# Attention and gated layer on one core: value products of 64 columns a head, two heads side by side in the array, x stored once

## Chip, cores and metric

The kernel runs on one core of a Trainium2 chip. The metric is the device time of one execution, in microseconds (us).

## What is computed

A relative-position attention over 4 batches, 8 heads, 576 positions and 64 values a head, and then a gated layer on its output, all in float32:

```python
# q, k, v: (4, 8, 576, 64)
scores = q @ k.T / 8 + bias        # bias: (8, 576, 576), a small network of the positions
attn = exp(scores - max); attn = attn / (sum(attn) + 1e-9)
x = (attn @ v).transpose(0, 2, 1, 3).reshape(2304, 512)
out = (sigmoid(x @ w_gate) * (x @ w_val)) @ w_out     # d_ff = 1536
```

## The kernel before

It has three stages one behind the other: the bias tables (to about 120 us), the attention (120 to 380 us), and the gated layer in two forms, three-term products for the first 768 tokens (380 to 535 us) and sums of seven products for the rest (535 to the end). Numbers that need more than one pass of the array are split into an upper and a lower part.

**The attention** runs over 16 units; a unit u is a pair of heads p of one batch b. Each unit has nine steps s, and the loop variable n counts steps over all units (n = 9u + s). `score(n)` makes two heads' scores in the even steps (L627, each head on 64 of the array's 128 rows) and the last 64 rows of both heads in step 8 (L616). `soft` takes the scores out of PSUM with the bias on VectorE (L643) and makes the exponential `en` on ScalarE (L648). `turn` brings `en` into `at`, transposed and split into two float16 parts: four blocks of the first head over TensorE and PSUM (L672, split by ScalarE L561 and VectorE L562), four of the second (`CROSS`, steps 1, 3, 5, 7) over GpSimd, which splits them into `cr` (L555, L666), and a transposing DMA on SP's queue (L667). `crp` holds three `cr` buffers. GpSimd also splits the next unit's k and q (L555, L566). `tail` in step 3 does the last 64 columns and, in `normal`, sends the row sums out (`rt`, L696).

**The value products** of a unit are done while the next unit runs. `products(u)` yields 36 matmuls: for each head and each half of the 576 rows nine with a stationary operand of 128 columns, 64 of the upper part of v and 64 of its lower part, so that `acc` holds two halves which have to be added. `FILL` says how many are taken in each step. ScalarE copies `acc` to `xe` (L736) and SP stores it to `xs` in DRAM, both halves (L741). `split_v` makes v's parts, the upper on ScalarE (L602), the lower on VectorE from two SBUF operands (L603), in the steps `VSTEP`.

**Around the change** the order on each engine is the order of the program (`manual_schedule`): SP takes its DMAs one behind the other and waits at each for what it needs. A transposing DMA of the block that is turned in step t is issued in step t + 2 + `XLAG`. What has to be loaded again is put in `loads` and issued a step or two later. From unit 12 on `Moe.ahead` slips loads and preparation of x for the gated layer into the steps (`PLAN`).

**The gated layer** loads x back from `xs`. For tokens below 768 `load_x` brings both halves and `prep_x` adds them (L900). For the others `x_do` loads one half ("l") and adds the other by a DMA that accumulates, issued by GpSimd ("+", L1057).

Of the kernel before, what the change touches and what calls it, by code (L numbers as in the profile page):

```python
# [22 lines left out]
NA = S // 4  # L23
HF = S // 2
NCH = S // 64
FILL = (0, 6, 3, 6, 3, 6, 3, 6, 3)
ENB = 11
WM = 6
LAG, WSTEP, VSTEP, TAIL = 2, 2, (5, 7), 3
KSTEP, QSTEP = 1, 4  # L30
EARLY = 2
YPOS = [18, 22, 26, 30, 34, 38, 46, 52, 57, 62, 67, 72], [3, 9, 15, 21, 27, 33, 39, 45, 52, 58, 66, 72]
# [46 lines left out]
TURN = (0, 0), (1, 0), (0, 1), (1, 1), (0, 2), (1, 2), (0, 3), (1, 3)  # L79
CROSS = (1, 3, 5, 7)  # L80
TERMS = (0, 0), (0, 1), (1, 0)
XLAG = 3
XE = True, True
UP = 14
VCHUNK = (3, 4, 5, 6, 7)
# [86 lines left out]
@with_exitstack  # L172
def tile_kernel(ctx, tc, q, k, v, small, w_gate, w_val, w_out, steps, lpos, xtab, lx, out, phases="0AB"):
    nc = tc.nc
    dram = ctx.enter_context(tc.tile_pool(name="dram", bufs=1, reuse_waits="tile", space=bass.MemoryType.DRAM))
    xs = dram.tile([H * 2 * D, NT], F32, name="xs")
    rs = dram.tile([H, NT], F32, name="rs")
    scratch = dram.tile([3 * DFF // 128, 128, 4, 128], F32, name="scratch")

    moe = Moe(tc, w_gate, w_val, w_out, scratch, xs, rs, out)  # L180
    with ExitStack() as right, ExitStack() as att:
        pool = lambda n, st, side: st.enter_context(tc.tile_pool(name=n, bufs=1, side=side, reuse_waits="tile"))
        first = right.enter_context(ExitStack())
        keep = pool("keep", att, "left")
        over = pool("over", first, "right")
        biasL = keep.tile([128, NP, S], F32, name="biasL")
        ident = keep.tile([128, 128], F32, name="ident")
        make_identity(nc, ident)
        biases = over.tile([128, 24, S], F32, name="bias0"), keep.tile([128, 8, S], F32, name="bias3")

        def extra(n):
            n -= 9 * B * (NP - 1)
            if n == EARLY:
                first.close()
                moe.early(right)
            if n >= EARLY:
                moe.ahead(n)

        sizes = {}
        attn = attention(tc, att, q, k, v, biases, biasL, ident, xs, rs, sizes, extra)  # L200
        next(attn)
        with tc.manual_schedule():
            bias(tc, v, small, steps, lpos, xtab, lx, biases, biasL, ident, keep, sizes, moe, lambda: next(attn))
        if "A" in phases:
            for _ in attn:
                pass
            att.close()
# [309 lines left out]
def attention(tc, att, q, k, v, biases, biasL, ident, xs, rs, sizes, extra):  # L517
# [9 lines left out]
    yield  # L527


    units = [(p, b) for p in range(NP) for b in range(B)]  # L530
    qkraw, vraw, vsplit = {}, {}, {}

# [18 lines left out]
    load_q(0)  # L551
    load_v(0)
    yield
    def copy(dst, src):
        nc.gpsimd.tensor_scalar(out=dst, in0=src, scalar1=1.0, scalar2=1.0, op0=ALU.mult, op1=ALU.mult)  # L555

    def half(ap):
        return ap.rearrange("p (a b) -> p a b", a=2)

# [29 lines left out]
    st = pool("st", 4)  # L589
    rtp = pool("rtp", 2)  # L590
    atp = pool("atp", 2)
    crp = pool("crp", 3)
    xep = pool("xep", 2)
    ps_t = pool("ps_t", 3, space=PSUM)
    ps_v = pool("ps_v", 1, space=PSUM)
    ps_s = pool("ps_s", 2, space=PSUM)

    def split_v(u, h):
        if h == 0:
            vsplit[u] = vp.tile([128, 2, 5, 2, D], F16, name="vv")  # L600
        t, vv = vraw[u][:, h], vsplit[u][:, h]
        nc.scalar.activation(out=vv[:, :, 0], in_=t, func=AF.Copy, scale=sizes["up"])  # L602
        return lambda: nc.vector.scalar_tensor_tensor(out=vv[:, :, 1], in0=t, scalar=sizes["up"], in1=vv[:, :, 0], op0=ALU.mult, op1=ALU.subtract)  # L603

    state = {}

# [83 lines left out]
    def normal(u, pt):  # L690
        p, b = units[u]
        nc.tensor.transpose(pt[0:9, 2], state[u][0], ident)
        rt = rtp.tile([9, 128], F32, name="rt")

        def leave():
            nc.vector.tensor_scalar(out=rt, in0=pt[0:9, 2], scalar1=sizes["out"][0:9], scalar2=None, op0=ALU.mult)  # L696
            to = rs[2 * p:2 * p + 2, S * b:S * b + S]
            nc.sync.dma_start(out=to[:, 0:512].rearrange("h (i p) -> h i p", p=128), in_=rt[0:8])
            nc.sync.dma_start(out=to[:, 512:576].rearrange("(o h) p -> o h p", o=1), in_=rt[8:9].rearrange("o (h p) -> o h p", h=2))

        return leave
# [10 lines left out]
    def products(u):  # L712
        p, b = units[u]
        sm, at, ens = state[u]
        for h in range(2):
            xe = xep.tile([128, S], F32, name="xe")
            for e in range(2):
                cs = slice(HF * e, HF * e + HF)
                if u < NU - 1:
                    acc = ps_v.tile([128, 512], F32, name="acc")  # L720
                else:
                    if e == 0:
                        pair = ps_s.tile([128, 2, 512], F32, name="sc")
                    acc = pair[:, e]
                vv = vsplit[u][:, h]
                mms = []
                for J in range(4):
                    w = vv[:, J].rearrange("p s d -> p (s d)")
                    mms += [(w, at[:, h, J, cs]), (w, at[:, h, 5 + J, cs])]
                mms.append((vv[:, 4].rearrange("p s d -> p (s d)"), at[:, h, 4, cs]))  # L730
                for i, (l, r) in enumerate(mms):
                    nc.tensor.matmul(out=acc[:, 0:HF], lhsT=l, rhs=r, start=(i == 0), stop=(i == len(mms) - 1))  # L732

                    def leave(xe=xe, cs=cs, acc=acc, h=h, e=e):
                        if XE[e]:
                            nc.scalar.activation(out=xe[:, cs], in_=acc[:, 0:HF], func=AF.Copy)  # L736
                        else:
                            nc.vector.tensor_copy(out=xe[:, cs], in_=acc[:, 0:HF])
                        if e == 1:
                            r = D * (2 * p + h)  # L740
                            nc.sync.dma_start(out=xs[2 * r:2 * r + 2 * D, S * b:S * b + S], in_=xe)  # L741

                    yield leave if i == len(mms) - 1 else None

    NU = len(units)
    crossed = []
    with tc.manual_schedule():
        work = iter(())
        after, late, due, loads = [], [], [], []
        for n in range(9 * NU + LAG + 1):  # L750
# [27 lines left out]
                work = products(u - 1)  # L778
            if n == 9 * NU + LAG - 1:
                work = products(u - 1)  # L780
            for _ in range(FILL[s] if n < 9 * NU else 9 if n < 9 * NU + LAG else 0):
                f = next(work, None)
                if f:
                    f()
            if s in VSTEP and u < NU:
                late.append(split_v(u, VSTEP.index(s)))
                if s == VSTEP[1] and u + 1 < NU:
                    loads.append(lambda z=u + 1: load_v(z))
            extra(n)
        for f in after + late:  # L790
            f()
# [5 lines left out]
class Moe:  # L797
# [82 lines left out]
    def load_x(self, c, kc, eng=None):  # L880
        ts = slice(self.T * c, self.T * c + self.T)
        t = self.pools["xin"].tile([128, 2, self.T], F32, name="xin")
        for e in range(2):
            (eng or self.nc.sync).dma_start(
                out=t[64 * e:64 * e + 64],
                in_=self.xs[256 * kc + 128 * e:256 * kc + 128 * e + 128, ts].rearrange("(s p) t -> p s t", s=2))
        return t

    def load_r(self, c, kc, eng=None):
# [6 lines left out]
    def prep_x(self, c, t, r, hi, lo, kc):  # L896
        nc = self.nc
        x = t[:, 0]

        return [lambda: XENG(nc, c).tensor_tensor(out=x, in0=x, in1=t[:, 1], op=ALU.add),  # L900
                lambda: nc.vector.tensor_tensor(out=x, in0=x, in1=r, op=ALU.mult),
                lambda: nc.scalar.activation(out=hi[:, kc], in_=x, func=AF.Copy),
                lambda: nc.vector.tensor_tensor(out=lo[:, kc], in0=x, in1=hi[:, kc].bitcast(F32), op=ALU.subtract)]
# [115 lines left out]
    def x_do(self, q, w):  # L1019
# [8 lines left out]
            c, k = 2 * q + (n[2] == "2"), kc + 2 * (n[1] == "2")  # L1028
        if what == "l":
            t[n] = self.xtile(q)  # L1030
            self.load_half(nc.sync, t[n], c, k, 0)
        elif what == "r":
            t[n, "rec"] = self.load_r(c, k)
        elif what == "+":
            self.load_half(nc.gpsimd, t[n], c, k, 1, accum_op=ALU.add)
        elif what == "*":
            nc.vector.tensor_tensor(out=t[n], in0=t[n], in1=t.pop((n, "rec")), op=ALU.mult)
        elif what == "s":
# [11 lines left out]
            nc.scalar.activation(out=var[n][:, 0, kc], in_=t[n], func=AF.Copy, scale=self.up[q])  # L1050
        else:
            nc.vector.scalar_tensor_tensor(out=var[n][:, 1, kc], in0=t[n], scalar=self.up[q], in1=var[n][:, 0, kc], op0=ALU.mult, op1=ALU.subtract)  # L1052

    def load_half(self, eng, t, c, k, s, **how):
        for e in range(2):
            r = 256 * k + 128 * e + 64 * s
            eng.dma_start(out=t[64 * e:64 * e + 64], in_=self.xs[r:r + 64, self.T * c:self.T * c + self.T], **how)  # L1057
# [299 lines left out]
```

## Time and profile before

| | |
|---|---|
| three runs | 805.39, 801.32, 805.51 us; median 805.39 |
| the profiled execution | 800.84 us, its span 799.0 us |
| busy in the span | TensorE 735.8, VectorE 650.3, ScalarE 555.4, GpSimd 360.1 us |
| TensorE's granted clock | 0.987 of full speed |
| HBM | 80.80 MB read, 23.67 MB written |

A span is the time from the first to the last instruction, and 1.84 us of the execution lie outside it. Times inside the trace are counted from the span's start. The matmuls' ends are modelled, so that busy TensorE is not TensorE at its peak.

### The profile page before, as it was taken

Reading aid. Unit: us, or ns where it says so; the run is one execution under the profiler, and the core shown is the slowest. Engines: PE = TensorE matmul, PEld = TensorE weight load, DVE = VectorE, ACT = ScalarE, POOL = GpSimd, SP = SyncE. Lnnn points to the kernel's source line nnn. Section 1 sums busy time; section 2 is a strip of 40 time slices with the busy share of each in tenths; the row PEclk is TensorE's granted clock in tenths of the full one; section 3 lists DMA queues with packets and bytes.
Section 4 is the critical chain, followed back from the end, with each engine's and each line's share of the span. In section 5 each row is a group of like instructions: output and inputs, shape, how many; then the busy total and the mean of one; then the engine's idle time right before and its main releaser. Section 6 shows DMA issues by size and latency. Waiting matters only on the chain. (4 is left out here: it accounts for less than half of the span.)

```text
span 799.0 us, 17293 instructions
## 1 busy us (share of the span) xinstructions
PE 735.8 (92%) x6343; PEld 539.5 (68%) x6343; DVE 650.3 (81%) x1362; ACT 555.4 (70%) x1206; POOL 360.1 (45%) x451
## 2 busy tenths in 40 slices
PE   7999879888888988777999999998999999999997
PEld 4898867666766766565899899974555555555553
DVE  6788879888888889996498998878988886877762
ACT  5888738787887878776666666577666667666652
POOL 2245349788879986973001110046733221533100
PEclk9999988999999999999999999999999999999999
DMA  5487315878888798898989863357522211422102
GB/s 199 149 202 175 116 59 119 190 181 168 178 174 186 184 185 208 204 220 207 320 259 257 260 172 107 108 148 190 175 80 80 80 53 57 155 80 80 54 1 80
DMA packets 137237, 121.86 MB, mean 153 GB/s; under 512 B 82368, under 2 KB 106048, under 8 KB 137152
## 3 DMA queue, kind: packets, MB, share of 16 engines
q1 hardware_dynamic: 130560, 112.03, 51.5%
q0 software_dynamic: 4672, 5.77, 5.0%
q10 hardware_dynamic: 1920, 2.95, 1.1%
q8 instruction: 50, 0.82, 0.4%
q14 instruction: 35, 0.29, 0.1%
HBM read 80.80 MB, written 23.67 MB: 131 GB/s over the span
## 5 line engine op out<-in xcount | busy, mean ns | idle before, releaser
L1158 PEld LDWEIGHTS <-wv 128*128 128x128 f16 x1008 | 98.0, 98 | 85.5 <-issue 10.7
L648 ACT ACTIVATE en<-en,mn 128x576 f32<-128x576 f32 x144 | 110.8, 774 | 24.7 <-DVE mn L643 22.6
L1116 POOL TENSOR_TENSOR ws<-wm 128x256 f32<-128x256 f32 x44 | 42.4, 964 | 157.2 <-DMA wm<-scratch 109.0
L1158 PE MATMUL pg<-xq,wv 128*128 128x384 f16 x576 | 109.3, 326 | 3.3 <-ACT c L1184 2.4
L643 DVE CUSTOM_DVE_ANT_0 en<-sc,bias 128x576 f32<-128x576 f32 x128 | 91.9, 755 | 21.5 <-PE sc L627 19.1
L732 PE MATMUL acc<-at,vv 128*128 128x288 f16 x540 | 84.1, 288 | 19.4 <-DVE at L562 10.7
L666 POOL TENSOR_TENSOR cr<-en,cr 128x512 f16<-128x512 f32 (+1 forms) x128 | 97.1, 779 | 5.3
L627 PEld LDWEIGHTS sc<-k,part 64*128 64x128 f32 x768 | 58.5, 189 | 43.1 <-DVE mn L643 16.5
L627 PE MATMUL sc<-k,part 64*128 64x288 f32 x768 | 78.3, 317 | 10.0 <-DVE mn L643 8.1
L1005 PE MATMUL po<-wo,gh 128*128 128x512 f16 x288 | 85.7, 379 | 0.0
L1158 PE MATMUL pu<-xq,wv 128*128 128x384 f16 x432 | 82.0, 326 | 2.1 <-DVE c L1164 2.1
L1057 POOL DMA_DIRECT2D xt<-xs x32 | 27.0, 1085 | 108.7 <-DMA xt<-xs 108.7
L1164 DVE TENSOR_TENSOR c<-pu,c 128x384 f32<-128x384 f32 x72 | 40.0, 555 | 42.5 <-PE pu L1158 28.7
L562 DVE SCALAR_TENSOR_TENSOR at<-pt,at 128x512 f16<-128x512 f32 (+3 forms) x128 | 69.5, 564 | 5.8 <-ACT at L561 4.8
L561 ACT ACTIVATE at<-pt 128x512 f16<-128x512 f32 (+3 forms) x128 | 60.1, 496 | 19.9 <-PE pt L672 19.8
L732 PEld LDWEIGHTS <-vv 128*128 128x128 f16 x576 | 56.2, 98 | 25.0 <-issue 9.3
L427 PE MATMUL bps<-cfs,ind 128*128 128x64 bf16 x1458 | 67.5, 193 | 3.5 <-DVE bias L443 1.8
L408 ACT ACTIVATE ind<-y 128x576 bf16<-128x576 f32 x100 | 62.4, 651 | 10.8 <-PE y L403 8.0
L427 PEld LDWEIGHTS <-ind 128*128 128x128 bf16 x1458 | 58.7, 98 | 9.7 <-issue 3.0
L555 POOL TENSOR_SCALAR cr<-en 128x576 f16<-128x576 f32 x64 | 45.3, 708 | 43.9 <-DMA at<-cr 32.8
L1176 ACT ACTIVATE gh<-c 128x384 f16<-128x384 f32 x48 | 25.1, 523 | 54.1 <-DVE c L1174 52.5
L672 PE MATMUL pt<-ident,en 128*128 128x128 f32 x320 | 53.3, 291 | 6.5 <-ACT en L648 6.4
(179 smaller groups left out, 1757.3 us busy)
## 6 DMA issues: line engine op xcount, KB each, us to landing
wm<-scratch SPq DMA_DIRECT2D x48, 256.0 KB
xs<-xe SPq DMA_DIRECT2D x32, 288.0 KB
scratch<-wm SPq DMA_DIRECT2D x27, 256.0 KB
wo<-scratch SPq DMA_DIRECT2D x24, 256.0 KB
qr<-in_q_dram SPq DMA_DIRECT2D x16, 320.0 KB
vr<-in_v_dram SPq DMA_DIRECT2D x16, 320.0 KB
kr<-in_k_dram SPq DMA_DIRECT2D x16, 288.0 KB
xrec<-rs SPq DMA_DIRECT2D x48, 96.0 KB
```

Source lines behind the costliest of these rows:

```text
L408: nc.scalar.activation(out=o, in_=y[:, :, 0:HF], func=AF.Sigmoid, scale=float(2.0 ** 64))
L427: nc.tensor.matmul(out=o, lhsT=st, rhs=cfs[:, part], start=(part == 0), stop=(part == 2))
L561: nc.scalar.activation(out=hi, in_=ps, func=AF.Copy, scale=float(2.0 ** UP))
L562: return lambda: nc.vector.scalar_tensor_tensor(out=lo, in0=ps, scalar=float(2.0 ** UP), in1=hi, op0=ALU.mult, op1=ALU.subtract)
L627: nc.tensor.matmul(out=pair[h][:, e, 0:HF], lhsT=qs[rows, l, 128 * it:128 * it + 128], rhs=ks[rows, r, HF * e:HF * e + HF], start=(i == 0) ...
L643: nc.vector.tensor_tensor_reduce(out=half(en), in0=ps[:, :, 0:HF], in1=half(nbias), scale=-0.125, scalar=3.0e38, op0=ALU.add, op1=ALU.min, ...
L648: nc.scalar.activation(out=en, in_=en, func=AF.Exp, bias=mn, scale=-1.0, accum_out=sm)
L666: nc.gpsimd.tensor_tensor(out=t[:, a:a + z.stop - z.start], in0=en[:, z], in1=t[:, z], op=ALU.subtract)
L672: nc.tensor.transpose(pt[:, J], en[:, 128 * J:128 * J + 128], ident)
L732: nc.tensor.matmul(out=acc[:, 0:HF], lhsT=l, rhs=r, start=(i == 0), stop=(i == len(mms) - 1))
L1005: self.nc.tensor.matmul(out=po, lhsT=l[:, tt], rhs=r, start=(first and i == 0), stop=(last and i == 2))
L1158: nc.tensor.matmul(out=p, lhsT=W[i][:, l, at + kc], rhs=V[b][:, r, kc], start=(new and n == 0), stop=(n == 5), skip_group_check=not new)
```

## The change

The stationary operand of a value product has 64 columns, upper or lower part, and the two heads of a pair write to the partitions 0 to 63 and 64 to 127 of the same `acc`. The three terms upper by upper, upper by lower and lower by upper are added up in PSUM, so that `acc` is x itself for two heads. A unit now has 56 matmuls in 28 pairs (7 in each of the steps 1, 3, 5, 7), two copies to `xe` and one store. `xs` has half the rows; nothing is added in the gated layer. The lower part of v is taken by VectorE from the raw v in SBUF and the upper part in PSUM, which TensorE puts there by a product with a float16 identity (`lower_v`). `rt` is made by ScalarE. There are four `cr` buffers, the transposing DMAs are issued a step earlier, and v is loaded later.

```diff
-FILL = (0, 6, 3, 6, 3, 6, 3, 6, 3)
+FILL = (0, 7, 0, 7, 0, 7, 0, 7, 0)
-LAG, WSTEP, VSTEP, TAIL = 2, 2, (5, 7), 3
+LAG, WSTEP, VSTEP, TAIL = 2, 2, (3, 5), 3
-XLAG = 3
+XLAG = 2
-    xs = dram.tile([H * 2 * D, NT], F32, name="xs")
+    xs = dram.tile([H * D, NT], F32, name="xs")
+    eye = per.tile([128, 128], F16, name="eye")
+    copy(eye, ident)
-    crp = pool("crp", 3)
+    crp = pool("crp", 4)
-        nc.scalar.activation(out=vv[:, :, 0], in_=t, func=AF.Copy, scale=sizes["up"])
-        return lambda: nc.vector.scalar_tensor_tensor(out=vv[:, :, 1], in0=t, scalar=sizes["up"], in1=vv[:, :, 0], op0=ALU.mult, op1=ALU.subtract)
+        nc.scalar.activation(out=vsplit[u][:, h, :, 0], in_=vraw[u][:, h], func=AF.Copy, scale=sizes["up"])
+
+    def lower_v(u, h):
+        vv = vsplit[u][:, h]
+        pt = ps_t.tile([128, 4, 128], F32, name="pt").rearrange("p a b -> p (a b)")[:, 0:5 * D].rearrange("p (a b) -> p a b", a=5)
+        nc.tensor.matmul(out=pt, lhsT=eye, rhs=vv[:, :, 0], start=True, stop=True)
+        return lambda: nc.vector.scalar_tensor_tensor(out=vv[:, :, 1], in0=vraw[u][:, h], scalar=sizes["up"], in1=pt, op0=ALU.mult, op1=ALU.subtract)
-            nc.vector.tensor_scalar(out=rt, in0=pt[0:9, 2], scalar1=sizes["out"][0:9], scalar2=None, op0=ALU.mult)
+            nc.scalar.activation(out=rt, in_=pt[0:9, 2], func=AF.Copy, scale=sizes["out"][0:9])
...
+        vv = vsplit[u]
+        xe = xep.tile([128, S], F32, name="xe")
+        for e in range(2):
+            cs = slice(HF * e, HF * e + HF)
+            acc = ps_v.tile([128, 512], F32, name="acc")
+            mms = [(J, z, 5 * y + J) for J in range(4) for z, y in TERMS] + [(4, z, 4) for z in range(2)]
+            for i, (J, z, y) in enumerate(mms):
+                for h in range(2):
+                    nc.tensor.matmul(out=acc[D * h:D * h + D, 0:HF], lhsT=vv[:, h, J, z], rhs=at[:, h, y, cs],
+                                     start=(i == 0), stop=(i == len(mms) - 1))
...
+                        nc.sync.dma_start(out=xs[128 * p:128 * p + 128, S * b:S * b + S], in_=xe)
...
-                late.append(split_v(u, VSTEP.index(s)))
-                if s == VSTEP[1] and u + 1 < NU:
-                    loads.append(lambda z=u + 1: load_v(z))
+                upper_v(u, VSTEP.index(s))
+            if s - 2 in VSTEP and u < NU:
+                after.append(lower_v(u, VSTEP.index(s - 2)))
+            if s == 8 and u + 1 < NU:
+                loads.append(lambda z=u + 1: load_v(z))
...
+        (eng or self.nc.sync).dma_start(out=t[:, 0], in_=self.xs[128 * kc:128 * kc + 128, ts])
...
-        return [lambda: XENG(nc, c).tensor_tensor(out=x, in0=x, in1=t[:, 1], op=ALU.add),
+        return [lambda: None,
...
-            self.load_half(nc.gpsimd, t[n], c, k, 1, accum_op=ALU.add)
+            pass
```

TensorE's order in the middle of a unit before: the last two products of the first head (steps 4 and 5), the scores of step 6, the transposes of step 6, and the first product of the second head; [waits ...] are the semaphores of the engine or DMA waited for.

```order
L732 LDWEIGHTS vv
L732 MATMUL acc<-at,vv 128x288
L732 LDWEIGHTS vv
L732 MATMUL acc<-at,vv 128x288 [waits DVE_49]
L627 MATMUL sc<-k,part 128x288 [waits PE_49] x2
L627 MATMUL sc<-k,part 128x288 x10
L672 MATMUL pt<-ident,en 128x128 [waits Activation_49]
L672 MATMUL pt<-ident,en 128x128 x3
L732 LDWEIGHTS vv [waits DMAHW7_49,DMAHW6_49,DMAHW1_49]
L732 MATMUL acc<-at,vv 128x288 [waits Activation_49]
```

The same engine now, scores of step 2, transposes of step 2, the two small ones of `tail` in step 3, and the first two pairs of products.

```order
L633 MATMUL sc<-k,part 128x288 [waits DVE_49] x2
L633 MATMUL sc<-k,part 128x288 x10
L678 MATMUL pt<-ident,en 128x128 [waits Activation_49]
L678 MATMUL pt<-ident,en 128x128 x3
L692 MATMUL pt<-ident,en 64x128
L698 MATMUL pt<-ident,sm 9x128 [waits DVE_49]
L729 LDWEIGHTS vv
L729 MATMUL acc<-at,vv 64x288 [waits Activation_49]
L729 LDWEIGHTS vv [waits DMAHW3_49,DMAHW2_49]
L729 MATMUL acc<-at,vv 64x288 [waits DMAHW1_49]
```

The product that waits for three transposing DMAs stood behind the scores of step 6 and stands now behind those of step 2; the product that waited for VectorE's part of `tail`, ahead of the scores of step 6, is now far from it.

SP's order in one unit before (numbers tell buffers apart: `cr_4921`, `cr_4979`, `cr_5032`, `cr_5093` are the second head's four blocks of one unit):

```order
L543 DMA qr_4984<-in_q_dram 128x640
L741 DMA xs_57<-xe_4916 128x576
L667 DMA_TRANSPOSE at_4900<-cr_4921 128x9x128
L667 DMA_TRANSPOSE at_4900<-cr_4979 128x9x128
L548 DMA vr_5099<-in_v_dram 128x640
L667 DMA_TRANSPOSE at_4900<-cr_5032 128x9x128
L741 DMA xs_57<-xe_5027 128x576
L537 DMA kr_5152<-in_k_dram 128x576
L667 DMA_TRANSPOSE at_4900<-cr_5093 128x9x128
```

And now:

```order
L548 DMA qr_5100<-in_q_dram 128x640
L673 DMA_TRANSPOSE at_5014<-cr_5031 128x9x128
L673 DMA_TRANSPOSE at_5014<-cr_5095 128x9x128
L673 DMA_TRANSPOSE at_5014<-cr_5151 128x9x128
L553 DMA vr_5241<-in_v_dram 128x640
L735 DMA xs_57<-xe_5041 128x576
L542 DMA kr_5284<-in_k_dram 128x576
L673 DMA_TRANSPOSE at_5014<-cr_5217 128x9x128
```

The third block's transpose has moved ahead of the load of v, and one of the two stores is gone.

## Rows read from the trace of the kernel before

**Rows 1.** Windows by stage: length; busy us of PE, PEld, DVE, ACT, POOL; clock; DMA.

```profile
138.81:307.58 168.77, 149.15 (x1279) 115.72 (x1277) 148.79 (x387) 136.99 (x353) 141.08 (x174) 1.00 0.84 182
...
380.00:535.00 155.00, 153.99 (x811) 139.32 (x809) 127.71 (x251) 101.05 (x225) 22.38 (x26) 1.00 0.68 201
535.00:660.00 125.00, 119.54 (x663) 64.64 (x661) 108.65 (x177) 82.86 (x167) 54.34 (x59) 1.00 0.38 115
```

**Rows 2.** Step 8's scores in the timeline: start, us; units 1, 12 and 15.

```profile
138.81 1.06 PE L616 MATMUL sc<-k,part 128*128 128x288 f32 x6
...
307.58 1.06 PE L616 MATMUL sc<-k,part 128*128 128x288 f32 x6
...
360.01 1.06 PE L616 MATMUL sc<-k,part 128*128 128x288 f32 x6
```

**Rows 3.** Waits in the window 138.81 to 307.58, eleven units.

```profile
POOL cr L555 <- DMA at<-cr: 19.4, 10, 3.7
...
DVE en L643 <- PE sc L627: 14.4, 28, 0.6
...
PEld sc L627 <- DVE mn L643: 11.5, 23, 1.1
...
PE acc L732 <- DVE at L562: 6.4, 11, 0.6
...
PEld pt L672 <- issue: 3.7, 22, 0.2
...
PE acc L732 <- ACT xe L736: 3.2, 11, 0.3
```

**Rows 4.** Groups by shape in the same window: busy us, mean ns, idle before.

```profile
L562 DVE SCALAR_TENSOR_TENSOR at<-pt,at 128x512 f16<-128x512 f32 x44 | 29.8, 677 | 0.0
...
L603 DVE SCALAR_TENSOR_TENSOR vv<-vr,vup,vv 128x320 f16<-128x320 f32 x22 | 19.8, 900 | 0.4
...
L562 DVE SCALAR_TENSOR_TENSOR at<-pt,at 128x256 f16<-128x256 f32 x22 | 8.2, 415 | 0.0
...
L696 DVE TENSOR_SCALAR rt<-pt,vout 9x128 f32<-9x128 f32 x11 | 3.7, 339 | 0.4
```

**Rows 5.** Timeline 239 to 247 us: scores, products, VectorE's lower part beside GpSimd.

```profile
239.65 1.06 PE L627 MATMUL sc<-k,part 64*128 64x288 f32 x12
...
241.13 1.14 PE L732 MATMUL acc<-at,vv 128*128 128x288 f16 x8
...
245.72 1.56 POOL L566 TENSOR_TENSOR part<-qr,part 128x640 fp32r<-128x640 f32 x1
245.73 1.90 DVE L603 SCALAR_TENSOR_TENSOR vv<-vr,vup,vv 128x320 f16<-128x320 f32 x1
```

**Rows 6.** Source line L732, the products' matmuls and weight loads, ns min/median/max.

```profile
L732 PE MATMUL acc<-at,vv x399: 282/286/286, 138.5 to 307.6; 128*128 128x288 f16 x200
L732 PEld LDWEIGHTS <-vv x396: 95/98/98, 140.5 to 307.4; 128*128 128x128 f16 x198
```

**Rows 7.** A transposing DMA behind a load: SP's two rows, DMA busy in 131 to 135.

```profile
131.16 0.33 SPq L537 DMA_DIRECT2D kr<-in_k_dram  x1
131.54 1.48 SPq L667 DMA_TRANSPOSE at<-cr  x1
...
DMA  0000000000089946478979799999959999995200
```

**Rows 8.** Waits in the window 307.58 to 363.

```profile
PEld L732 <- DMA at<-cr: 4.4, 3, 3.3
```

**Rows 9.** Timeline at the end of the attention.

```profile
368.93 0.67 POOL L555 TENSOR_SCALAR cr<-en 128x576 f16<-128x576 f32 x1 [4.74 <-DMA at<-cr]
...
371.17 0.20 ACT L859 ACTIVATE sig<-sig 128x1 f32<-128x1 f32 x1 [2.02 <-POOL sig L858]
...
371.90 0.40 PE L732 MATMUL sc<-at,vv 128*128 128x288 f16 x1 [2.87 <-DVE at L562]
```

**Rows 10.** GpSimd's accumulating DMA issues in the gated layer.

```profile
L1057 POOL DMA_DIRECT2D xt<-xs x32 | 27.0, 1085 | 108.7 <-DMA xt<-xs 108.7
```

More of the change, by code (lines that the diff above doesn't have):

```diff
@@ L527, in attention, with copy @@
     yield
+    def copy(dst, src):
+        nc.gpsimd.tensor_scalar(out=dst, in0=src, scalar1=1.0, scalar2=1.0, op0=ALU.mult, op1=ALU.mult)
+    eye = per.tile([128, 128], F16, name="eye")
+    copy(eye, ident)
     units = [(p, b) for p in range(NP) for b in range(B)]
@@ L553, in attention @@
     yield
-    def copy(dst, src):
-        nc.gpsimd.tensor_scalar(out=dst, in0=src, scalar1=1.0, scalar2=1.0, op0=ALU.mult, op1=ALU.mult)
     def half(ap):
@@ L596, in attention, with upper_v @@
     ps_s = pool("ps_s", 2, space=PSUM)
-    def split_v(u, h):
+    def upper_v(u, h):
         if h == 0:
             vsplit[u] = vp.tile([128, 2, 5, 2, D], F16, name="vv")
-        t, vv = vraw[u][:, h], vsplit[u][:, h]
-        nc.scalar.activation(out=vv[:, :, 0], in_=t, func=AF.Copy, scale=sizes["up"])
-        return lambda: nc.vector.scalar_tensor_tensor(out=vv[:, :, 1], in0=t, scalar=sizes["up"], in1=vv[:, :, 0], op0=ALU.mult, op1=ALU.subtract)
+        nc.scalar.activation(out=vsplit[u][:, h, :, 0], in_=vraw[u][:, h], func=AF.Copy, scale=sizes["up"])
[4 more added lines that the diff above has]
+        return lambda: nc.vector.scalar_tensor_tensor(out=vv[:, :, 1], in0=vraw[u][:, h], scalar=sizes["up"], in1=pt, op0=ALU.mult, op1=ALU.subtract)
     state = {}
@@ L714, in products @@
         sm, at, ens = state[u]
[L715 to L743, printed above, removed]
@@ new lines, in products, with leave @@
+        vv = vsplit[u]
[8 more added lines that the diff above has]
+                                     start=(i == 0), stop=(i == len(mms) - 1))
+                def leave(cs=cs, acc=acc, e=e):
+                    nc.scalar.activation(out=xe[:, cs], in_=acc[:, 0:HF], func=AF.Copy)
+                    if e == 1:
+                        nc.sync.dma_start(out=xs[128 * p:128 * p + 128, S * b:S * b + S], in_=xe)
+                yield leave if i == len(mms) - 1 else None
@@ L780, in attention @@
                 work = products(u - 1)
-            for _ in range(FILL[s] if n < 9 * NU else 9 if n < 9 * NU + LAG else 0):
+            for _ in range(FILL[s] if n < 9 * NU else 14 if n < 9 * NU + LAG else 0):
                 f = next(work, None)
@@ L882, in load_x @@
         t = self.pools["xin"].tile([128, 2, self.T], F32, name="xin")
[L883 to L886, printed above, removed]
+        (eng or self.nc.sync).dma_start(out=t[:, 0], in_=self.xs[128 * kc:128 * kc + 128, ts])
         return t
@@ L1030, in x_do @@
             t[n] = self.xtile(q)
-            self.load_half(nc.sync, t[n], c, k, 0)
+            nc.sync.dma_start(out=t[n], in_=self.xs[128 * k:128 * k + 128, T * c:T * c + T])
         elif what == "r":
@@ L1052, in x_do @@
             nc.vector.scalar_tensor_tensor(out=var[n][:, 1, kc], in0=t[n], scalar=self.up[q], in1=var[n][:, 0, kc], op0=ALU.mult, op1=ALU.subtract)
[L1054 to L1057, printed above, removed]
     def xtile(self, q):
```

## The prediction

> **What bounds the kernel now.** I read the stages first, by the windows. From 380 us to the end TensorE is busy for 153.99 of 155.00 us and 119.54 of 125.00 [rows 1]: the gated layer can give back little more than the 6.5 us missing there. The attention is another matter: in eleven units TensorE, VectorE, ScalarE and GpSimd are busy for 149.15, 148.79, 136.99 and 141.08 of 168.77 us [rows 1], so no engine sets the pace alone. A unit lasts (307.58 - 138.81) / 11 = 15.34 us, and the last three together 360.01 - 307.58 = 52.43, which is 6.4 more than three of those [rows 2].
>
> Next the waits of those eleven units [rows 3]. VectorE waits 14.4 us for scores; the scores' weight loads wait 11.5 us for VectorE to free their PSUM. The two take turns, and what either does beside the scores makes the turn longer. On TensorE two waits belong to the value products: 6.4 us for `tail`'s last part by VectorE, once a unit, and 3.2 us for ScalarE's copy of the only `acc`. GpSimd waits for nobody but the transposing DMA that still reads a `cr` buffer, 19.4 us; without that it would need (168.77 - 19.4) / 11 = 13.6 us a unit. That is the floor under any gain here: 1.75 us a unit.
>
> Last the sizes on VectorE [rows 4]. The lower part of v takes 0.900 us, longer than the split of 512 columns out of PSUM, 0.677, though it has 320. The timeline shows why: one of them lasts 1.90 us, from 245.73, beside a GpSimd instruction that runs from 245.72 for 1.56 [rows 5].
>
> **The change, part by part, for one unit.**
>
> *TensorE, products.* Eight of today's products take 1.14 us, the last 0.286 long [rows 5, 6]: (1.14 - 0.286) / 7 = 0.122 us each, 36 of them 4.39. The 28 pairs have no row here. If the two of a pair run side by side for nothing, a pair costs 0.122; if one runs behind the other, 0.244. The nearest row is the scores, two heads in two halves of the array's rows: twelve in 1.06 us [rows 5]. One behind the other they would take 11 x 0.122 + 0.286 = 1.63, so they do run in pairs, at (1.06 - 0.286) / 5 = 0.154. Their operands are float32; I take 0.14, between 0.122 and 0.154, and 28 x 0.14 = 3.92: 0.47 less than now.
>
> *TensorE, additions.* Two products with the identity, 320 columns each, 2 x 0.122 x 320 / 288 = 0.27. Four more changes of the array's form, between transposes and products: transposes behind scores lose 3.7 / 22 = 0.17 each time [rows 3], 0.68 together. In all TensorE has 0.48 more work. But both waits go: the product that needs `tail` stands far behind it now, and between the two halves of `acc` lie two steps, so that the copy is done. That is 6.4 / 11 + 3.2 / 11 = 0.87 us [rows 3]. TensorE gains 0.39.
>
> *VectorE.* The lower part takes one operand from PSUM. Splits out of PSUM cost 0.415 us at 256 columns and 0.677 at 512 [rows 4], 1.02 ns a column, so 0.48 at 320: 2 x (0.900 - 0.48) = 0.84. `rt` leaves, 0.339. Together 1.18. The lower bound is nothing saved on the two lower parts, if GpSimd disturbs them all the same.
>
> *ScalarE* loses two copies and gets `rt`; it is the least busy of the four and I count nothing. The cover is its idle time, 168.77 - 136.99 = 31.8 us or 2.9 a unit [rows 1].
>
> *A unit.* If the smaller gain hides in the larger turn, only TensorE's 0.39 counts; if both lie in one chain, 1.57. As the two engines wait for each other about equally long, I take the middle, 1.0: 14.3 us a unit, above GpSimd's 13.6.
>
> *Late units.* Three of them, 3.0, and of the 6.4 us over, 4.4 are TensorE waiting for transposes [rows 8]. With a fourth `cr` buffer and without GpSimd's additions of x these should come earlier; I count half, 2.2. All of it is the upper bound, nothing the lower.
>
> *End of the attention.* GpSimd waits 4.74 us for a `cr` buffer there, the table load on ScalarE waits 2.02 behind it, and a product of TensorE 2.87 behind that [rows 9]. Four buffers remove this. On the other hand eighteen of the last products stand today behind the layer's first matmuls, which cover the landing of their transposes; now all products stand ahead of them and wait. I count 1 us, between a loss of 2 and a gain of 3.
>
> *Gated layer.* GpSimd's 32 accumulating issues, 27.0 us [rows 10], and the additions go, and half the bytes. GpSimd waits most of that stage; TensorE is full. I count 1 us of the missing 6.5; 0 to 3.
>
> *Sum.* Twelve units (the window's eleven and the one ahead of it) 12.0, late units 5.2, the end 1, the layer 1: 19.2. The profiled execution took 800.84 us, so 781.6. The three runs lie between 0.5 and 4.7 above it; I say **783**.
>
> **Rivals.**
>
> *Halves one behind the other.* Were a pair 0.244, TensorE would have 2.9 us more a unit than in my sum. Half to all of that would lengthen the turns, so a unit would be 15.8 to 17.2 us; with the middle 16.5, fifteen units cost 17.5 more than today, less the 4.2 at other places: 814, slower. It decides from 0.14 + 1.0 / 28 = 0.176 us a pair on. Against it: the scores' 0.154. For it: that is a split of the rows, and each half reads its own 64 partitions, while here both halves read all 128.
>
> *Weight loads that stick out.* Today's loads, 98 ns each [rows 6], lie under the product ahead of them, or nine products would not come 0.122 apart. If the loads of a pair could not be hidden under the pair ahead, one of them exposed would make a pair 0.24 and the unit as long as above: 814 too. The Trainium skill speaks for this one: TensorE: Matmul & The Clock Gate, section Part 3 (Packing small matmuls), says that a load runs under a matmul in flight only where the row group differs, and column halves share all rows. By that rule today's products would not hide theirs either, and rows 6 say that they do; so I give it little.
>
> *Transposes that come late.* The third block's transpose was issued in step 10 and needed in step 15 of the same count; now it is issued in step 9 and needed in step 12. At 1.70 us a step that was 8.5 us; at 1.59 it is 4.8. Behind one load a transpose lands 3.3 us after its issue: SP's row begins at 131.54 and the DMA engines are busy until 134.8 [rows 7]. That leaves 1.5. Two transposes stand ahead of it on SP's queue, and the DMA share is 0.84 [rows 1]: where it comes 1 us late, TensorE stands in front of its first products, the next scores wait behind them, and a unit's gain is gone. What stays is 2.2, 1 and 1 at the other places, or 797. For it: in the late units such waits exist already, 3.3 us at once [rows 8]. Against it: one store of 288 KB fewer a unit, the load of v out of the way, and a GpSimd that doesn't wait.
>
> *More than I count.* If both gains lie in one chain, 1.57 a unit for fifteen, 23.6, and with 4.4, 3 and 2 at the other places 33: 768. GpSimd's floor allows it.
>
> **How the numbers follow.** My forecast 0.60; more than that 0.13; late transposes 0.12; halves one behind the other 0.09; loads that stick out 0.06. The first lies between 772 and 792. The range is 766 to 803: it takes in the larger gain and the late transposes and leaves out the two slow cases, 0.15, and little else. Less than 0.5% (4 us) can't be told from no change here. Faster: 0.60 + 0.13 and a small part of the late transposes, 0.75. Same: the rest of them, 0.10. Slower: 0.15.
>
> **What would show it.** Pairs: 14 products in the steps 1, 3, 5, 7 within 1.0 to 1.3 us from first to last start; 1.7 or more means no pairs. The lower part: 0.5 us, never 1.9. No wait of a product for VectorE's `tail`, none for `xe`; none of GpSimd for `cr`. Step 8's scores 14.3 us apart. A wait of the first product of step 3 for the transposing DMA in every unit would show the third rival, and would make me wrong.

## The result, and the profile after

| | before | after |
|---|---|---|
| median of the runs | 805.27 us (801.32 to 805.51) | 792.35 us (791.77 to 794.64) |
| ratio, 95% interval | | 0.9856, 0.982 to 0.9893 |
| span of the profiled execution | 799.0 us | 790.1 us |
| mean of eleven units | 15.34 us | 14.57 us |
| the three late units together | 52.43 us | 54.01 us |

The change makes the kernel 12.9 us faster by the medians and 8.9 by the two profiled executions; forecast were 19.2 and 783 us. The place of the difference is read from the scores of step 8, as in [rows 2]: the twelve units that were summed take 174.6 us in place of 184.2 (9.5 less, forecast 12.0), the three late ones 1.6 more (forecast 5.2 less), and from there to the end of the span it is 1.2 less (forecast 2). So of the 10 us that are missing some two thirds (6.8) were to come from the late units, 2.5 from the steady ones and 0.8 from what lies behind.

The windows of the changed kernel, eleven units and then the three late ones; they answer to [rows 1]:

```profile
core 0: us, PE busy (x) PEld busy (x) DVE busy (x) ACT busy (x) POOL busy (x), PEclk, DMA share, GB/s
138.00:298.30 160.30, 146.56 (x1521) 112.34 (x1520) 139.86 (x375) 133.87 (x342) 140.12 (x178) 1.00 0.85 171
298.30:352.31 54.01, 44.39 (x417) 33.31 (x416) 44.58 (x112) 39.04 (x99) 35.71 (x45) 0.91 0.80 172
```

VectorE lost 8.9 us of work against [rows 1], TensorE 2.6 in spite of the products with the identity. The groups of the same eleven units show the new shapes; they answer to [rows 4]:

```profile
L729 PE MATMUL acc<-at,vv 128*64 128x288 f16 x617 | 49.9, 289 | 7.8 <-DMA at<-cr 6.3
...
L609 DVE SCALAR_TENSOR_TENSOR vv<-vr,vup,pt 128x320 f16<-128x320 f32 x22 | 11.9, 540 | 0.3
...
L702 ACT ACTIVATE rt<-pt,vout 9x128 f32<-9x128 f32 x11 | 3.8, 342 | 0.0
```

The lower part takes 0.540 us in place of 0.900. And the waits, which answer to [rows 3]:

```profile
engine line waited for: us in total, times, longest us
PEld L729 <- issue: 15.6, 58, 1.5
POOL cr L531 <- ACT en L654: 14.4, 20, 1.4
...
DVE en L649 <- PE sc L633: 11.7, 20, 1.6
...
PE acc L729 <- DMA at<-cr: 6.3, 9, 1.3
PEld L729 <- DMA at<-cr: 2.9, 2, 1.6
```

The two waits of the products for `tail` and for `xe` are gone, and GpSimd waits for ScalarE, no longer for the transposing DMA. What is new is the wait of the products for that DMA: 6.3 us, in nine of the eleven units. The 2.9 us of the weight loads are not to be added, for both of those waits stand at the same moments as waits of the products (at 189.66 and 249.04 us); where an expectation below speaks of 9.2 us, it counts them twice. One unit in order of time shows where the wait comes from:

```profile
start us, us, engine line op out<-in xcount [idle before <-releaser]
211.35 5.57 SPq L673 DMA_TRANSPOSE at<-cr  x3
...
217.76 0.27 PE L698 MATMUL pt<-ident,sm 128*9 128x128 f32 x1
...
219.61 1.02 PE L729 MATMUL acc<-at,vv 128*64 128x288 f16 x13 [1.16 <-DMA at<-cr]
...
221.75 0.76 DVE L649 CUSTOM_DVE_ANT_0 en<-sc,bias 128x576 f32<-128x576 f32 x1 [1.59 <-PE sc L633]
...
222.73 0.77 ACT L654 ACTIVATE en<-en,mn 128x576 f32<-128x576 f32 x1
...
223.49 0.77 ACT L654 ACTIVATE en<-en,mn 128x576 f32<-128x576 f32 x1
...
224.25 0.34 ACT L702 ACTIVATE rt<-pt,vout 9x128 f32<-9x128 f32 x1
...
224.62 0.63 SPq L704 DMA_DIRECT2D rs<-rt  x1
...
225.13 0.75 PEld L729 LDWEIGHTS <-vv 128*64 128x64 f16 x14 [0.17 <-issue]
225.13 1.05 PE L729 MATMUL acc<-at,vv 128*64 128x288 f16 x14
...
226.42 5.57 SPq L673 DMA_TRANSPOSE at<-cr  x3
```

Seven pairs of products take 1.05 us (at 225.13), so a pair costs (1.05 - 0.286) / 6 = 0.127 us: the heads do run side by side. Three transposes leave SP in one block of 5.57 us, at 211.35 and again at 226.42, each time behind a store of `rt`, for the second block the one at 224.62. That store is late because `rt` is: it comes at 224.25, although its transpose is done at 218.03, since on ScalarE it stands behind exponentials (222.73 and 223.49). Behind the block of 211.35 the products of step 3 wait 1.16 us, until 219.61; the scores stand behind them, and VectorE waits 1.59 us for the scores. What SP itself waits for in the eleven units:

```profile
SPq L704 <- ACT xe L733: 34.7, 11, 4.2
```

In the kernel before this row read as follows; with two small ones for the other two units it makes 14.7 us:

```profile
SPq L698 <- DVE at L562: 13.7, 9, 2.7
```

The worst place is the first late unit, 298.30 to 319.10, where SP has the loads of x between its transposes:

```profile
300.31 1.35 SPq L673 DMA_TRANSPOSE at<-cr  x1
301.71 1.24 SPq L886 DMA_DIRECT2D xrec<-rs  x2
303.05 1.30 SPq L673 DMA_TRANSPOSE at<-cr  x1
304.40 0.59 SPq L879 DMA_DIRECT2D xin<-xs  x1
305.09 1.49 SPq L673 DMA_TRANSPOSE at<-cr  x1
...
305.40 0.28 PE L729 MATMUL acc<-at,vv 128*64 128x288 f16 x1
308.87 1.89 PE L729 MATMUL acc<-at,vv 128*64 128x288 f16 x13 [3.19 <-DMA at<-cr]
310.68 1.81 PE L633 MATMUL sc<-k,part 64*128 64x288 f32 x12
```

The third block's transpose is issued at 305.09, 0.3 us before the products that read it; TensorE stands for 3.19 us, and comes back at the lower of its two clocks (a granted clock of 0.50 from 310 to 313 us): 1.89 us for 13 products, 1.81 for scores that take 1.06 otherwise. The granted clock of the whole unit is 0.84.

### The profile page after: what moved, and what is told of

It reads as the page before. It is cut to its first block, busy times and chain, and to the rows that moved or that the text cites. A ratio compares the mean times of both kernels' runs of the same rounds, so it can differ in the third digit from the quotient of the medians.

```text
span 790.1 us, 17816 instructions
## 1 busy us (share of the span) xinstructions
PE 735.1 (93%) x6695; PEld 537.6 (68%) x6695; DVE 631.6 (80%) x1342; ACT 549.6 (70%) x1190; POOL 326.3 (41%) x416
## 4 chain that ended last, share of the span: by engine, by line
PE 53%; DMA 11%; ACT 7%; DVE 5%; POOL 5%; issue 3%; SPq 1%; ACTq 0%; POOLq 0%; DVEq 0%
PE po L998 16%; PE pg L1146 10%; DMA at<-cr 8%; PE pu L1146 7%; PE pg L974 6%; PE pu L974 6%; PE acc L729 4%; ACT en L654 3%; POOL cr L672 2%; PE sc L633 2%; ACT at L563 2%; PE pt L678 2%; POOL cr L531 1%; DMA wo<-scratch 1%; DVE wv L1115 1%
## 5 line engine op out<-in xcount | busy, mean ns | idle before, releaser
L1104 POOL TENSOR_TENSOR ws<-wm 128x256 f32<-128x256 f32 x44 | 44.3, 1006 | 296.5 <-DMA xt<-xs 158.7
L672 POOL TENSOR_TENSOR cr<-en,cr 128x512 f16<-128x512 f32 (+1 forms) x128 | 93.0, 748 | 5.4
L729 PE MATMUL acc<-at,vv 128*64 128x288 f16 x896 | 77.0, 304 | 16.4 <-DMA at<-cr 13.7
L633 PE MATMUL sc<-k,part 64*128 64x288 f32 x768 | 76.3, 318 | 3.3 <-DVE bias L443 1.8
L729 PEld LDWEIGHTS <-vv 128*64 128x64 f16 x896 | 52.1, 115 | 34.9 <-issue 25.4
L531 POOL TENSOR_SCALAR cr<-en 128x576 f16<-128x576 f32 x64 | 43.0, 672 | 39.3 <-ACT en L654 30.8
L974 PE MATMUL pg<-xhi,w 128*128 128x384 f32 x192 | 54.0, 339 | 1.2 <-ACT g L983 1.2
```

The source lines that it names most:

```text
L633: nc.tensor.matmul(out=pair[h][:, e, 0:HF], lhsT=qs[rows, l, 128 * it:128 * it + 128], rhs=ks[rows, r, HF * e:HF * e + HF], start=(i == 0) ...
L672: nc.gpsimd.tensor_tensor(out=t[:, a:a + z.stop - z.start], in0=en[:, z], in1=t[:, z], op=ALU.subtract)
L729: nc.tensor.matmul(out=acc[D * h:D * h + D, 0:HF], lhsT=vv[:, h, J, z], rhs=at[:, h, y, cs], start=(i == 0), stop=(i == len(mms) - 1))
L974: self.nc.tensor.matmul(out=(pg, pu)[z], lhsT=l, rhs=r, start=(kc == 0 and i == 0), stop=(kc == 3 and i == 2))
```

## The experiments

Theory A: the third block of the second head comes too late for the products of step 3, which wait for it, and this takes back a part of what the change gives. A1: it comes late because SP stands in front of the store of `rt`. A2: three steps are too few for a transpose in any case. Theory B: the wait only takes the place of waits for VectorE and GpSimd. The table has all runs; each ratio is taken against runs of the kernel before made at the same time, whose medians go from 803.4 to 805.4 us; the unit is the mean of the same eleven, "late" the three after them, by the scores of step 8 in each profile.

| run | median us | ratio to before, 95% | unit | late |
|---|---|---|---|---|
| after | 792.4 | 0.9856 (0.982 to 0.9893) | 14.57 | 54.0 |
| e1 columns 256 + 320 | 782.6 | 0.9744 (0.9716 to 0.9771) | 13.96 | 50.9 |
| e2 store of rt later | 780.7 | 0.9723 (0.9696 to 0.9751) | 13.99 | 49.3 |
| e3 rt on VectorE | 785.0 | 0.977 (0.9745 to 0.9795) | 14.24 | 50.8 |
| e4 lower part from SBUF | 791.9 | 0.9862 (0.9835 to 0.9888) | 14.37 | 53.7 |
| e5 = e1 + e2 | 777.4 | 0.9661 (0.9628 to 0.9694) | 13.94 | 51.2 |
| e6 = e2, heads in turn | 813.3 | 1.0093 (1.0064 to 1.0122) | 16.58 | 51.3 |
| e7 before + 4 cr buffers | 794.0 | 0.9863 (0.9832 to 0.9894) | 14.85 | 51.5 |
| e8 = e5, 3 cr buffers | 782.8 | 0.9728 (0.9694 to 0.9762) | 14.02 | 51.6 |
| e9 = e5 + e3 | 776.7 | 0.966 (0.9644 to 0.9676) | 13.76 | 48.5 |
| e10 = e5 + e4 | 786.7 | 0.9782 (0.976 to 0.9804) | 14.16 | 50.5 |
| e11 = e5, store later still | 778.3 | 0.9681 (0.9663 to 0.9699) | 13.86 | 47.4 |
| e12 before + lower part | 804.0 | 0.9999 (0.9979 to 1.0018) | 14.89 | 60.8 |

**e1, the third block read later.**

```diff
-            cs = slice(HF * e, HF * e + HF)
+            cs = slice(256 * e, 256 + 320 * e)
...
```

> The changed kernel (792.4 us), with the query columns cut into 256 and 320 instead of 288 and 288: the first half of the products then needs only the first two transposed blocks of the second head, the third one two steps of products later. Nothing else moves. Theory A, the products now stand before a transpose that comes late: the wait of the first products of step 3 for the transposing DMA (9.2 us in eleven units) is gone, a unit falls from 14.57 to 13.9 or 14.0 us, the thirteenth unit loses most of its 20.8 (3.2 and 3.6 us of waits and the slower clock behind them), the time is 779 to 785. Theory B, that wait only stands where TensorE would wait for VectorE or GpSimd anyway: unit 14.4 to 14.6, time 789 to 793.

Measured: 782.6, unit 13.96. The products' wait for the DMA falls from 6.3 us to 1.3, that of the weight loads from 2.9 to 1.4:

```profile
PEld L730 <- DMA at<-cr: 1.4, 3, 0.7
PE acc L730 <- DMA at<-cr: 1.3, 4, 0.4
```

A holds, B does not: the eleven units are 6.8 us shorter, about as much as the wait was long.

**e2, the store of rt behind the third transpose.** `leave` only makes `rt`; its two stores are put on a list and issued after the transpose of step 0 of the next unit.

```diff
...
+            if s == 0 and kept:
+                kept.pop(0)()
```

> The changed kernel, but the two stores of rt are put on the SP queue after the third transpose of the unit instead of ahead of the first. In the changed kernel SP stands 34.7 us of eleven units in front of these stores, because ScalarE makes rt late, and then issues three transposes in a row. Theory A1, SP's queue held by rt is why the transposes come late: SP's wait goes, the products' wait for the DMA goes with it, unit 13.9 to 14.1, time 780 to 786. Theory A2, three steps are too few for a transpose even on a free queue: the products still wait some 9 us in eleven units, time 789 to 793.

Measured: 780.7, unit 13.99. The waits of the eleven units, and SP's timeline in one of them:

```profile
PE acc L735 <- DMA at<-cr: 1.4, 4, 0.5
```

```profile
232.97 5.39 SPq L673 DMA_TRANSPOSE at<-cr  x3
```

A1 holds: the same three steps are enough. SP still issues three transposes in a row here, but it is done with them at 238.36, 2.9 us after the scores of step 8 at 235.47; in the changed kernel that was 231.99 after 226.15, 5.8 us. Over all twelve units it is 1.9 to 3.7 us here and 4.0 to 6.0 there.

**e3, rt on VectorE again.**

```diff
-            nc.scalar.activation(out=rt, in_=pt[0:9, 2], func=AF.Copy, scale=...)
+            nc.vector.tensor_scalar(out=rt, in0=pt[0:9, 2], scalar1=..., scalar2=None, op0=ALU.mult)
```

> The changed kernel with rt made on VectorE again, as before. Theory A1, ScalarE's late rt holds the SP queue: SP waits less for it (14.7 us in eleven units before, 34.7 now), the products wait less than half of 9.2 us; VectorE pays 0.34 us a unit for it; together 786 to 791. Theory B, moving rt was a plain saving of 0.34 us of VectorE: 794 to 798.

Measured: 785.0, below what either theory gave. The waits of the eleven units:

```profile
PE acc L729 <- DMA at<-cr: 3.7, 9, 0.9
```

The products' wait falls to 3.7 us, but SP still stands 32.2 us in front of the store, 2.5 less than in the changed kernel: A1's sign for SP hardly came. How long SP stands is not the measure. `rt` comes 4.3 to 5.1 us after its transpose here, 4.9 to 6.3 in the changed kernel, and SP is done with the third transpose 3.4 to 5.9 us after the scores of step 8, in the middle 4.5, between the 5.1 of the changed kernel and the 2.8 of e2. That this order is also the order of the waits (6.3, 3.7 and 1.4 us) fits A1. Moving `rt` to ScalarE cost 0.9% here, 7 us, where the sum had 0.34 us a unit of gain.

**e4, the lower part from SBUF.** The identity's product is left out and `in1` is the upper part in SBUF.

> The changed kernel without the products with the identity: the lower part of v is taken from the upper part in SBUF again, all else stays. By my sum VectorE loses 0.36 to 0.42 us on each of two lower parts a unit and TensorE gains 0.27 and some 0.4 of form changes; if VectorE's part of the turn counts more, unit 14.7 to 14.9 and 795 to 798; if the two cancel, 790 to 794; if TensorE is what counts, 784 to 789. The lower part itself: 0.85 to 0.95 us a mean, with single ones near 1.9.

Measured: 791.9, no difference to the changed kernel. But the lower part takes 0.640 us, not 0.9, so the experiment took away less than it was meant to:

```profile
L607 DVE SCALAR_TENSOR_TENSOR vv<-vr,vup,vv 128x320 f16<-128x320 f32 x22 | 14.1, 640 | 0.0
```

**e5, e1 and e2 together.**

> Columns cut into 256 and 320 and the stores of rt behind the third transpose, both at once. If both only take away the same wait for the transposes (9.2 us in eleven units), they do not add: unit 13.9 to 14.0, 777 to 783, within 4 us of the better of the two. If SP's queue and the need are two separate losses, they add: unit below 13.7, 770 or less.

Measured: 777.4, 3.3 us below e2 by the medians, and 0.6% by the ratios; unit 13.94, and 13.70 in seven of the eleven. In the steady units they are two remedies for one loss and don't add. The profiled execution was the longest of its six, 782.4, so it doesn't show where the 3 us come from.

**e6, the heads one behind the other.** This is e2 with another order: in each half of the columns all products of the second head go ahead of those of the first, still fourteen a step.

```diff
...
-            for i, (J, z, y) in enumerate(mms):
-                for h in range(2):
+            for m in range(len(mms)):
+                for h, i in [divmod(2 * m + j, len(mms)) for j in range(2)]:
+                    h, (J, z, y) = 1 - h, mms[i]
...
```

> The kernel with the late stores of rt (780.7 us), its 28 pairs of products of a unit taken apart: all products of the second head ahead of all of the first, so that neighbours in the queue use the same half of the array's columns, fourteen a step as before. Theory, the pairs run side by side and pay for the change: fourteen products take 13 x 0.122 + 0.286 = 1.87 us in place of 1.05, TensorE gets 3.3 us a unit more, half to all of which lengthens the unit: 15.6 to 17.3 us, 800 to 830. Rival, two products in different column halves only share the cost of their loads and the order does not matter: 1.05 to 1.2 us for fourteen, 779 to 784.

Measured: 813.3, 32.6 us above e2, 2.6 a unit. The timeline of TensorE:

```profile
230.49 1.90 PE L736 MATMUL acc<-at,vv 128*64 128x288 f16 x14
```

Fourteen products take 1.90 us where they took 1.05. With the heads one behind the other the changed kernel is 0.9% slower than the kernel before, even with e2's edit; that neighbours in the queue use different halves of the columns carries the change.

**e7, the kernel before with a fourth cr buffer.**

```diff
-XLAG = 3
+XLAG = 2
-    crp = pool("crp", 3)
+    crp = pool("crp", 4)
```

> The kernel before with nothing but the fourth cr buffer and the transposes issued a step earlier. If GpSimd's 19.4 us of waits for cr in eleven units were a wait beside the turn of TensorE and VectorE, as my sum has it: its waits move to ScalarE's exponentials, unit 15.2 to 15.4, 801 to 806 with a little from the late units. If they held the unit: 14.0 to 14.9 and 787 to 798, and most of the gain of the whole change is this line.

Measured: 794.0, ratio 0.9863: two lines give as much as the whole change. The sum had priced them at nothing in a unit. The products wait for `tail` and for the copy to `xe` as before (6.3 and 3.2 us), and yet the unit falls by 0.49. SP stands 30.6 us in front of the store of `rt` here, with no product waiting for a transpose. Among the groups of VectorE the largest difference is to this row of [rows 4]:

```profile
L603 DVE SCALAR_TENSOR_TENSOR vv<-vr,vup,vv 128x320 f16<-128x320 f32 x22 | 13.7, 625 | 0.4
```

The lower part, from SBUF as ever, takes 0.625 us in place of 0.900, 6.1 us less in eleven units, which are 5.4 us shorter. It is not the only difference: the addition to the row sums (`sm`), which also has two operands in SBUF, takes 2.6 us more (0.498 in place of 0.268 each), so VectorE's busy time falls by 2.9 us alone. So a new theory, C: GpSimd's waits cost little themselves; they put its instructions beside VectorE's lower part. This run alone does not show it.

**e8, three buffers and transposes a step later on e5.**

> Columns 256 and 320 and late stores of rt, but three cr buffers and the transposes a step later, as in the kernel before. If the fourth buffer is worth what GpSimd waited (19.4 us in eleven units, 1.75 a unit): unit 14.6 to 15.5 and 790 to 805. If its worth lies in the late units and at the end alone: unit 13.9 to 14.1, 781 to 788. If it is worth nothing: within 2 us of the same kernel with four.

Measured: 782.8, ratio 0.9728 against 0.9661. With the lower part from PSUM the unit is 14.02, not 14.6 or more: in steady units the fourth buffer is worth next to nothing there. But GpSimd waits little for `cr` in these eleven units, where it was 19.4 us in the kernel before:

```profile
POOL cr L531 <- DMA at<-cr: 4.8, 9, 1.6
```

So the run does not show what 19.4 us of waiting would cost. Some 5 us remain by the medians, which the two profiles, with spans of 781.0 and 780.6, do not show; where they lie stays open.

**e9, rt on VectorE on e5.**

> Columns cut and late stores of rt (777.4 us), and rt on VectorE again. Now nothing on SP hangs on rt, so only its cost as work is left. If its 0.34 us on VectorE counts as in my sum (a part of the turn): steady unit 13.70 to 13.85 - 14.05, and 779 to 783. In the last three units TensorE waits 8 us in all for ScalarE's rt, which holds a bank; if that outweighs it: late units 51.2 to 47 - 49, and 772 to 777.

Measured: 776.7, unit 13.76, late units 48.5: the second reading came. (The 8 us of waits that it names are weight loads and transposes at the same three moments, 4.6 us at most.) VectorE's 0.34 us cost nothing. It has the lowest median of all, at 0.966 (0.9644 to 0.9676), which can't be told from e5.

**e10, the lower part from SBUF on e5.**

> Columns cut and late stores of rt (777.4 us), and the lower part of v from SBUF, without the products with the identity. Where the transposes were late this changed nothing (791.9 to 792). If that was because those waits covered it, and the lower part is a gain as in my sum: steady unit 13.70 to 13.9 - 14.2, 780 to 785. If the products with the identity and their changes of form (some 0.7 us) cancel VectorE's gain (0.64 to 0.54 us twice): 775 to 780. If they cost more: below 775.

Measured: 786.7 and 0.9782 against 0.9661, so the lower part from PSUM is worth 1.2%, some 9 us, where transposes come in time. Where they lie is not all shown: the two profiled executions differ by 4.4 us, 3.5 more in the twelve summed units and 2.0 more behind the late ones, where no lower part is made. Four cr buffers are there, and still the lower part is slow again. Its group, and then the timeline:

```profile
L607 DVE SCALAR_TENSOR_TENSOR vv<-vr,vup,vv 128x320 f16<-128x320 f32 x22 | 20.3, 920 | 0.0
```

```profile
235.65 1.67 POOL L670 TENSOR_TENSOR cr<-en,cr 128x512 f16<-128x512 f32 x2
235.92 1.23 DVE L607 SCALAR_TENSOR_TENSOR vv<-vr,vup,vv 128x320 f16<-128x320 f32 x1
```

It begins inside GpSimd's instruction and takes 1.23 us. In e4 GpSimd was done, or nearly, when it began:

```profile
236.09 1.44 POOL L670 TENSOR_TENSOR cr<-en,cr 128x512 f16<-128x512 f32 x2
...
237.31 0.56 DVE L607 SCALAR_TENSOR_TENSOR vv<-vr,vup,vv 128x320 f16<-128x320 f32 x1
```

And from PSUM, in e5, the same neighbour does not disturb it:

```profile
218.79 1.43 POOL L672 TENSOR_TENSOR cr<-en,cr 128x512 f16<-128x512 f32 x2
219.07 0.54 DVE L609 SCALAR_TENSOR_TENSOR vv<-vr,vup,pt 128x320 f16<-128x320 f32 x1
```

Taken one by one, the 22 lower parts of each run say the same. In the kernel before 14 begin with more than 0.4 us of a GpSimd instruction still to run, and each takes what is left of it and 0.34 or 0.35 us more, 0.76 to 1.90 in all; in e7 2 of 22 begin so, in e4 3, in e10 11. In e5 20 begin so, and each takes 0.54 or 0.55 us.

**e11, the stores of rt behind the fourth transpose.** `s == 2` in place of `s == 0` in the edit of e2.

> Columns cut, and the stores of rt put two steps further back, behind the fourth transpose of a unit, so that the load of v no longer stands behind them. If ScalarE's wait for v in the late units (2.1 us) and the stores ahead of the fourth transpose count: 51.2 us of late units to 47 - 50, 773 to 777. If not: 776 to 781. Steady units stay at 13.7.

Measured: 778.3. The late units fall to 47.4 us as the first theory has it, the time does not fall with them. What takes it back stays open.

**e12, the lower part alone in the kernel before.** The functions `upper_v` and `lower_v` of the change with its steps of v; three buffers, full products.

> The kernel before with one part of the change alone: the lower part of v from PSUM by products with the identity, and the steps of v with it; three cr buffers, transposes issued late, full products, rt on VectorE. GpSimd still waits for cr. Theory C, what the fourth buffer alone gained (11.4 us) was that VectorE's lower part no longer stood behind GpSimd's instructions (0.900 us there, 0.625 with the fourth buffer): the lower part is 0.54 us, unit 15.34 to 14.7 - 14.9, 794 to 799 though GpSimd's waits for cr stay. Theory D, GpSimd's waits themselves held the unit: unit 15.2 to 15.5 and 802 to 808, with the 0.5 us a unit of TensorE's added work.

Measured: 804.0, no change: the time is what theory D gave, the unit what theory C gave. In its parts this is C for the steady units and a loss behind them. The waits, the group and the window of the first late unit (eleven units are 138.49 to 302.25, 14.89 each), and the waits in that window:

```profile
POOL cr L557 <- DMA at<-cr: 20.7, 9, 3.4
```

```profile
L609 DVE SCALAR_TENSOR_TENSOR vv<-vr,vup,pt 128x320 f16<-128x320 f32 x22 | 11.7, 534 | 0.0
```

```profile
302.25:327.89 25.64, 17.58 (x121) 12.79 (x119) 14.76 (x37) 13.24 (x35) 18.34 (x22) 0.80 0.96 213
```

```profile
ACT vv L603 <- DMA vr<-in_v_dram: 4.4, 1, 4.4
...
PE acc L738 <- DMA at<-cr: 3.4, 1, 3.4
```

GpSimd waits as long as ever, and the unit is 0.45 us shorter: its waiting did not hold the unit, and the lower part is what is left as the cause, though the edit also moves the steps of v. The first late unit then takes 25.6 us at a clock of 0.80 and gives all of it back. TensorE waits 3.4 us in it for a transpose that SP issues behind loads, and ScalarE 4.4 us for the load of v, with TensorE's product for the lower part 2.6 us behind it. So the later load of v has a part in it; how large a one was not tried.

## Why the prediction came out as it did

**Pairs: right, and a little better.** 0.127 us where 0.14 was taken; the sign of 1.0 to 1.3 us for fourteen products holds to the end of the last, 1.05, while its start comes after 0.76. e6 shows the price of the other case, a unit of 16.58 where the rival had 15.8 to 17.2. The weight loads don't stick out: fourteen of them take 0.75 us under products of 1.05. The Trainium skill's page TensorE: Matmul & The Clock Gate, section Part 3 (Packing small matmuls), whose rule that a load overlaps products in flight only where the row group differs would have had them exposed, does not fit this trace.

**Waits of the products for `tail` and `xe`: right.** Both rows are gone, and so is GpSimd's wait for `cr` in the eleven units.

**The lower part: nearly right in size, wrong in what it depends on.** It takes 0.54 us for 0.48, and never more than 0.55. The gain of 0.36 a piece is there only where the lower part meets GpSimd: 0.900 and 0.920 us in two kernels that read SBUF, 0.625 and 0.640 in two others. The sum took the 0.900 for a property of the instruction beside GpSimd's load; it is one of the phase between two engines. The Trainium skill says this in SBUF — State Buffer, section Who interferes with whom: a VectorE instruction with two inputs in SBUF and a GpSimd one that reads SBUF contend for a shared port pair, which is an exclusive lock. The trace agrees: 1.23 us where most of GpSimd's instruction is still to run, 0.56 where little of it is, and 0.54 beside it with one input in PSUM.

**The fourth buffer: the sum's largest blind spot.** It counted nothing for it in a unit, since GpSimd waited for nobody's work; e7 measures 11.4 us by the medians for it and the earlier transposes. It and the lower part look like two ways out of the same collision: each alone brings the unit of the kernel before to 14.9 (e7, e12), and with the lower part from PSUM the fourth buffer adds nothing to a steady unit (e8), so they are not to be added. That the collision is all that e7 takes away is argued, not shown: VectorE's busy time fell by 2.9 of the 5.4 us.

**`rt` on ScalarE: the term with the wrong sign.** "I count nothing", with 2.9 us of idle time a unit as the cover. ScalarE had the time, but not at that moment: `rt` came 4.9 to 6.3 us after its transpose, where it was 3.9 in the kernel before, and SP, which issues in order, stood with three transposes behind its store. Idle time covers the work of a step, not its lateness. e3 puts the price at 7 us, a part of the loss told next and not one beside it, for in e9, where nothing waits for `rt`, its place makes no difference that can be told from e5.

**Late transposes: the rival with 0.12, which came in part.** Its sign, a wait of the first products of step 3 for the transposing DMA, is there in nine of eleven units, so this step of the forecast was wrong though the time lay in the range. It named the two transposes ahead of the third one on SP's queue and took no time for them: the block of three takes SP 5.57 us in the unit shown, the two ahead some 3.7 of them (an estimate, two thirds), and 1.5 us were to spare. It cost 9 to 11 us (1.1 and 1.3% by e1 and e2), not the whole gain: 6.4 to 6.8 in the eleven units, 3.1 to 4.7 in the late ones. This is also the step that failed in the late units: 5.2 us were counted there as gain, since x needs no additions and a buffer more, and the first of them alone took 20.8 us. With the transposes in time the late units are 47.4 to 51.2, a gain of 1 to 5.

**The end of the attention and the gated layer: small, and not to be read from one profile.** 2 us were counted and 1.2 came. But from the last scores of step 8 to the end of the span the changed kernel and its ten variants take 436.1 to 440.1 us, though none of them edits that layer. So a few us of difference in the whole time need not come from the steps that an experiment edits.

So the forecast of faster held and the time lay in the range, but two errors of opposite sign stand behind it: 9 to 11 us lost at the transposes, which were not in the sum, and a steady unit that without this loss falls to 13.94, 1.4 less than before, where 1.0 was taken. That the second makes up for a part of the first is luck.

## What to carry to other kernels

When a result moves to an idle engine, ask when that engine reaches it in its queue and what stands behind its store on the issuing queue; the idle share says nothing of either. A VectorE instruction with both inputs in SBUF has no fixed price beside a busy GpSimd (0.54 to 1.90 us for one and the same here): before counting its measured mean as a gain, see whether it overlaps GpSimd's rows, since any edit that shifts the two engines can give the same gain for nothing. Where a change reads something earlier, cut the work so that the part that comes last is read last, as 256 + 320 columns do here. Waits of weight loads and of products at the same moment are one wait and are counted once.

## What the hardware showed that was not expected

Products of 64 columns in different halves of the array's columns overlap almost wholly: 0.127 us a pair, against 0.122 for one full product of the same 288 columns. The weight loads, 0.109 us each on average, run two at a time under them. A wait of TensorE of 3.19 us for one DMA cost more than itself: the granted clock was 0.50 behind it, and 13 products took 1.89 us, where 13 take 1.02 in a steady unit. A lower part from SBUF that began inside a GpSimd instruction took what was left of that one and 0.35 us; from PSUM it took 0.54 or 0.55 us beside the same instructions.
